# Cosine attention and a gated feed-forward on one core: batch 2's preparation moved into chunk 0's second product, and three evictions moved between ScalarE and VectorE

## The chip, the cores and the metric

The kernel runs on one core of a Trainium2 chip. The metric is device time in microseconds, the median over runs of one program. Each of the core's engines works through its own queue in order: TensorE (PE; its weight loads are PEld), VectorE (DVE), ScalarE (ACT), GpSimd (POOL, which here issues the loads and clears small pieces), and SyncE (SP, which issues the stores and the transposing DMAs).

## The reference

```python
def _attn_ref(q, k, v):                       # 8 batches, 8 heads, 576 positions, 64 wide
    theta = np.pi / 2.0 * pos / S
    q_p = phi(q, cos_w, sin_w)                # relu(q)*cos next to relu(q)*sin: 128 wide
    k_p = phi(k, cos_w, sin_w)
    kv = np.einsum('bhsf,bhsd->bhfd', k_p, v)
    z = np.sum(k_p, axis=2)
    num = np.einsum('bhsf,bhfd->bhsd', q_p, kv)
    den = np.einsum('bhsf,bhf->bhs', q_p, z)[..., None] + 1e-06
    return num / den

def _moe_ref(x, w_in, w_out):                 # x: the 4608 tokens, 512 wide
    h = x @ w_in                              # 512 x 2048
    return (h * np.cos(h)) @ w_out            # 2048 x 512
```

## The kernel before

**Tiling.** The 4608 tokens go through the feed-forward in nine chunks of 512 (`NCHUNK`). A chunk has a first product of 16 groups (`m1_group`: four matmuls into M, then ScalarE's `co` = sin(M + pi/2) and VectorE's `g` = M * co) and a second product of 4 tiles of 128 tokens, each in four parts of four matmuls (`m2_part`; after the last part ScalarE copies the tile to `ost`, and SP stores it). Chunk 0 does its first product in two halves of 256 tokens. A batch has 576 tokens, so chunk 1 needs all of batch 0 and most of batch 1.

**Attention** is done batch by batch, a little ahead of the chunk that needs it:

- `loads(b)`: three DMAs from POOL into q16, k16, v16 (two buffers each)
- `scaled(b, which, i)`: two VectorE instructions per sixth i, relu and times cos or sin, into `kp` or `qp` (one buffer each)
- `spread_v`: four ScalarE copies that lay v out with a column of ones, `vz`, which POOL sets first (batches from 1 on)
- `kv_head`: six matmuls per head into KV; ScalarE copies four heads at a time to `kvz`
- `q_turn`: turns qp into `X`. For batches 0 and 1 by matmuls into `QT` that ScalarE copies out (batch 1: two sixths at a time); for later batches by a transposing DMA on SP
- `num_tile(b, t)`: eight matmuls into `NP` for 128 tokens, then VectorE's dn, rd and x
- `x_turn(b, t)`: turns x into `XT`, the input of the first product; by matmuls into `XP` and a ScalarE copy for batches 0 and 1, by a transposing DMA for later ones

**The order** is written out by hand. `at(c, s, f, ...)` puts a step behind place s of chunk c; places 0 to 15 are the first product and 16 to 31 the second (chunk 0: 0 to 31 and, from z = 32 on, 32 to 47). Every engine's queue holds its instructions in that order. Before the first chunk stands a prologue with the whole of batch 0's preparation; in it, matmuls on zeros (`warm`, tile W) stand between steps.

**Buffers in PSUM.** Pool `psA` has two buffers for KV, QT of batch 1, NP and XP of batch 1 (tag "att"); pool `psM` has two for tag m1 and two for m2, for M, for QT and XP of batch 0 and for the tiles of the second product. Which buffer an allocation gets, and so for whom it waits, is settled when the program is built.

Of the kernel before, what the change touches and what calls it, by code (L numbers as in the profile page):

```python
# [10 lines left out]
AF = mybir.ActivationFunctionType  # L11
ALU = mybir.AluOpType
F32 = mybir.dt.float32
F16 = mybir.dt.float16
# [3 lines left out]
def kernel(  # L18
# [9 lines left out]
    nc = tc.nc  # L28
    B, H, S, D = q.shape
    Dm, Dff = moe_w_in.shape  # L30
    P = 128
    F = 2 * D
    R = 6
    PR = S // R
# [4 lines left out]
    NCHUNK = NTOK // CH  # L39
    NSUB = CH // P  # L40
# [18 lines left out]
    psA = ctx.enter_context(tc.tile_pool(name="psA", bufs=2, space=bass.MemoryType.PSUM))  # L59
    psM = ctx.enter_context(tc.tile_pool(name="psM", bufs=2, space=bass.MemoryType.PSUM))  # L60

    CS = cpool.tile([PR, 2, R], F32, name="CS")
# [37 lines left out]
    def scaled(b, which, i, h0=0, h1=H):  # L100
        s = st[b]
        if which + "p" not in s:
            s[which + "p"] = apool.tile([PR, R, H * F], F16, name=which + "p",
                                        tag=which + "p", bufs=1)
        dst = s[which + "p"][:, i].rearrange("p (h t d) -> p h t d", t=2, d=D)
        src = s[which + "16"][:, 0:H * RUN].rearrange("p (h i d) -> p h i d", i=R, d=D)
        for t in range(2):
            nc.vector.tensor_scalar(  # L108
                out=dst[:, h0:h1, t, :], in0=src[:, h0:h1, i, :],
                scalar1=0.0, scalar2=CS[:, t, i:i + 1],  # L110
                op0=ALU.max, op1=ALU.mult,
            )

    def q_turn(b, i, tag="m1"):
        s = st[b]
        if i == 0:
            s["X"] = apool.tile([P, H, S], F16, name="X", tag="X")
        if b >= 2:
            nc.sync.dma_start_transpose(
                out=s["X"][:, :, i * PR:(i + 1) * PR], in_=s["qp"][:, i],  # L120
            )
            return
        if b == 1:
            if i % 2 == 0:
                s["QT"] = psA.tile([P, 2, H, P], F16, name="QT", tag="att")
            QT = s["QT"][:, i % 2]
        else:
            QT = psM.tile([P, H, P], F16, name="QT", tag=tag)
        for h in range(H):
            nc.tensor.matmul(  # L130
                QT[:, h, 0:PR], lhsT=s["qp"][:, i, h * F:(h + 1) * F], rhs=ID[0:PR, 0:PR],
                is_transpose=True,
            )
        if b == 1 and i % 2 == 0:
            return
        i0 = i - (b == 1)
        dst = s["X"][:, :, i0 * PR:(i + 1) * PR]
        if b == 1:
            nc.scalar.activation(
                out=dst.rearrange("p h (a c) -> p a h c", a=2),  # L140
                in_=s["QT"][:, :, :, 0:PR], func=AF.Copy,
            )
        else:
            nc.scalar.activation(out=dst, in_=QT[:, :, 0:PR], func=AF.Copy)  # L144

# [64 lines left out]
    def x_turn(b, t):  # L210
        x = st[b]["x", t]
        new = min(P, S - t * P)
        n0 = b * S + t * P
        if b >= 2:
            nc.sync.dma_start_transpose(out=XT[:, :, n0:n0 + new], in_=x[P - new:P, :])
            return
        if b == 0:
            XPf = psM.tile([P, 1024], F16, name="XP", tag="m1")
        else:
            XPf = psA.tile([P, 2048], F16, name="XP", tag="att")  # L220
        XP = XPf[:, 0:NCT * P].rearrange("p (i c) -> p i c", c=P)
        for i in range(NCT):
            nc.tensor.matmul(  # L223
                XP[:, i], lhsT=x[:, i * P:(i + 1) * P], rhs=ID,
                is_transpose=True,
            )
        nc.scalar.activation(out=XT[:, :, n0:n0 + new], in_=XP[:, :, P - new:P], func=AF.Copy)  # L227
# [19 lines left out]
    def m2_part(c, m, part):  # L247
        if part == 0:
            tag = "m1" if c == 0 and m >= 2 else "m2"
            st["m2", m] = psM.tile([P, Dm], F32, name="M2", tag=tag)  # L250
        M2 = st["m2", m]
        for j in range(4 * part, 4 * part + 4):
            nc.tensor.matmul(  # L253
                M2, lhsT=st["g", c][:, j, m * P:(m + 1) * P], rhs=w_out_sb[:, j],
                start=(j == 0), stop=(j == NJT - 1),
            )
        if part < 3:
            return
        ost = opool.tile([P, Dm], F32, name="ost", tag="ost")
        nc.scalar.activation(out=ost, in_=M2, func=AF.Copy)  # L260
        n = c * CH + m * P
        r = 0
        while r < P:
            b, rem = divmod(n + r, S)
            i, p = divmod(rem, PR)
            cnt = min(P - r, PR - p)
            rows = out[b * S:(b + 1) * S, :].rearrange("(p i) d -> p i d", i=R)
            nc.sync.dma_start(out=rows[p:p + cnt, i, :], in_=ost[r:r + cnt, :])
            r += cnt
# [3 lines left out]
    def at(c, s, f, *args):  # L273
        plan.setdefault((c, s), []).append((f, args))

    HS = NJT
    M2S = NJT
# [6 lines left out]
    def plan_stage0():  # L284
        at(0, 1, q_turn, 0, 4)
        at(0, 2, x_turn, 0, 2)
        at(0, 3, q_turn, 0, 5)
        at(0, 6, num_tile, 0, 3)
        at(0, 10, num_tile, 0, 4)
        at(0, 12, x_turn, 0, 3)  # L290
        at(0, HS, x_turn, 0, 4)
        z = 2 * HS
        for i in range(R):
            at(0, z + i // 2, scaled, 1, "k", i)
            at(0, z + 4 + i // 2, scaled, 1, "q", i)
        for n in range(4):
            at(0, z + 1 + n, spread_v, 1, 2 * n)
        for h in range(H):
            at(0, z + 4 + h // 4, kv_head, 1, h)
        for i, n in enumerate((6, 6, 7, 7, 8, 8)):  # L300
            at(0, z + n, q_turn, 1, i)
        for n, f, t in ((9, num_tile, 0), (10, num_tile, 1), (11, x_turn, 0),
                        (11, num_tile, 2), (12, x_turn, 1), (13, num_tile, 3),
                        (14, x_turn, 2), (15, x_turn, 3), (16, num_tile, 4)):
            at(n // 16, n % 16 + (0 if n > 15 else z), f, 1, t)
        at(1, 3, x_turn, 1, 4)
        for i in range(R):
            at(i // 3, i % 3 + (0 if i > 2 else z + 13), scaled, 2, "q", i)
            at(i // 3, i % 3 + (0 if i > 2 else z + 13), q_turn, 2, i)

    def plan_ahead(c, b):
        for i in range(R):
            at(c, M2S + 1 + 2 * i, scaled, b, "q", i)
            at(c, M2S + 1 + 2 * i, q_turn, b, i)
        for i in range(R):
            if i < 3:
                at(c, M2S + 10 + 2 * i, scaled, b, "k", i)
            else:
                at(c + 1, 2 * i - 5, scaled, b, "k", i)
        for n in range(4):  # L320
            at(c, M2S + 8 + 2 * n, spread_v, b, 2 * n)
        for h in range(H):
            at(c + 1, 12 + h // 4, kv_head, b, h)

    def plan_tiles(c, b, s0):
        for t in range(NT):
            at(c, s0 + 2 * t, num_tile, b, t)
            at(c, s0 + 2 * t, x_turn, b, t)

    plan_stage0()  # L330
    at(1, 0, loads, 3)
    for i in range(R):
        at(1, 3 + 2 * i, scaled, 2, "k", i)
    for n in range(4):
        at(1, 2 + 3 * n, spread_v, 2, 2 * n)
    for h in range(H):
        at(1, 14 + h // 4, kv_head, 2, h)
    at(1, M2S, loads, 4)
    plan_tiles(1, 2, M2S + 2)
    plan_ahead(1, 3)  # L340
    for c in range(2, NCHUNK):
        if c + 3 < B:
            at(c, 12, loads, c + 3)
        if c + 1 < B:
            plan_tiles(c, c + 1, M2S)
        if c + 2 < B:
            plan_ahead(c, c + 2)
# [5 lines left out]
    with tc.manual_schedule():  # L353
# [24 lines left out]
        def warm(n):  # L378
            for _ in range(n):
                nc.tensor.matmul(W, lhsT=WU[:, 0:P], rhs=WU, start=True, stop=True)  # L380

        warm(29)
        for i in range(R):
            scaled(0, "k", i, 0, 4)
        for i in range(2):
            scaled(0, "q", i)
            q_turn(0, i)
            warm(2)
        for i in range(R):
            scaled(0, "k", i, 4, 8)  # L390
        for h in range(4):
            kv_head(0, h)
        warm(2)
        for h in range(4, 8):
            kv_head(0, h)
        for i in range(2, 4):
            scaled(0, "q", i)
            q_turn(0, i, ("m1", "m2")[i % 2])
        warm(1)
        num_tile(0, 0)  # L400
        warm(2)
        num_tile(0, 1)
        warm(3)
        x_turn(0, 0)
# [6 lines left out]
        for s in range(2 * HS):  # L411
            n = s // HS * (CH // 2)
# [45 lines left out]
```

## Time and profile before

| | |
|---|---|
| median of 3 runs | 307.33 us (307.19 to 307.38) |
| the profiled execution | 307.16 us |
| its span | 305.4 us |
| PE, DVE, ACT busy | 293.5, 192.4, 164.6 us |
| first matmul of chunk 0's first product (L234) | 20.13 us |
| first matmul of chunk 0's second product (L253) | 38.73 us |
| first matmul of chunk 1's first product | 59.54 us |
| end of it in the chain of waits | 78.19 us |
| last eviction (L260) | 300.92 us |

Times are microseconds from the start of the span. A line such as L234 is a line of the kernel before. A group "out<-in" names tiles: `M<-XT,w_in_sb` is the first product, `M<-w_out_sb,g` the second. A wait names what released the instruction last. In the chain of waits each step is what the next one waited for, so only work in the chain sets the end.

### The profile page before, as it was taken

The numbers are of one execution on the slowest core, as the hardware profiler recorded it, in microseconds if no ns is written. First come the engines' busy times: TensorE is split into PE (matmuls) and PEld (weight loads), VectorE is DVE, ScalarE is ACT, GpSimd is POOL, SyncE is SP. The second block draws the span as 40 slices with busy tenths as digits, with TensorE's granted clock in tenths as the row PEclk, the third lists the DMA queues.
The fourth block names the chain that finished last, engine by engine and source line by source line (L and its number), as shares of the span: only waits on it lengthen the run. The fifth ranks groups of instructions, "written<-read, shape, count | busy, mean of one in ns | idle before, by whom it ended". The sixth has DMA issues, their size and how long they took to land.

```text
span 305.4 us, 5574 instructions
## 1 busy us (share of the span) xinstructions
PE 293.5 (96%) x2101; PEld 153.6 (50%) x2101; DVE 192.4 (63%) x486; ACT 164.6 (54%) x261; POOL 29.1 (10%) x47
## 2 busy tenths in 40 slices
PE   8799999898999999999999999999999999999994
PEld 3567856444554554455445544554455444444441
DVE  2868892599459778577757775777576257108600
ACT  1268956587246735673567256725672167227511
POOL 8433103010101201020102000000000000000000
PEclk9999999999999999999999999999999999999999
DMA  7999999997999976996699676228621520121022
GB/s 99 193 205 206 204 205 204 240 205 103 144 167 145 217 130 140 177 173 118 138 155 204 109 121 146 63 43 125 148 57 36 121 63 0 34 69 38 0 69 69
DMA packets 73483, 38.81 MB, mean 127 GB/s; under 512 B 46320, under 2 KB 68848, under 8 KB 73456
## 3 DMA queue, kind: packets, MB, share of 16 engines
q0 software_dynamic: 23856, 18.35, 40.9%
q1 hardware_dynamic: 49600, 20.10, 32.2%
q8 instruction: 16, 0.26, 0.3%
q14 instruction: 11, 0.09, 0.1%
HBM read 36.74 MB, written 9.44 MB: 151 GB/s over the span
## 4 chain that ended last, share of the span: by engine, by line
PE 84%; DVE 9%; DMA 2%; ACT 2%; issue 1%; POOL 0%; ACTq 0%; POOLq 0%
PE M L253 40%; PE M L234 33%; DVE g L243 6%; PE KV L165 4%; PE NP L191 3%; DMA q<-in_q_dram 2%; PE QT L130 1%; ACT co L240 1%; DVE kp L108 1%; PE W L380 1%; DVE x L204 1%; PE KV L175 1%; DVE qp L108 1%; ACT XT L227 1%; PE XP L223 0%
## 5 line engine op out<-in xcount | busy, mean ns | idle before, releaser
L243 DVE TENSOR_TENSOR g<-M,co 128x512 f16<-128x512 f32 (+1 forms) x160 | 99.5, 634 | 64.5 <-ACT co L240 64.3
L253 PE MATMUL M<-w_out_sb,g 128*128 128x512 f16 x576 | 132.4, 379 | 0.1
L234 PE MATMUL M<-XT,w_in_sb 128*128 128x512 f16 (+1 forms) x640 | 130.2, 358 | 2.3 <-ACT XT L227 1.5
L240 ACT ACTIVATE co<-M,PIH 128x512 f32<-128x512 f32 (+1 forms) x160 | 101.9, 644 | 28.0 <-PE M L234 26.7
L234 PEld LDWEIGHTS <-w_in_sb 128*128 128x128 f16 x640 | 61.5, 98 | 62.4 <-issue 4.3
L253 PEld LDWEIGHTS <-g 128*128 128x128 f16 x576 | 53.6, 98 | 58.2 <-issue 0.3
L260 ACT ACTIVATE ost<-M 128x512 f32<-128x512 f32 x36 | 21.5, 597 | 86.3 <-PE M L253 72.8
L108 DVE TENSOR_SCALAR kp<-k,CS 96x512 f16<-96x512 f16 (+1 forms) x108 | 30.4, 348 | 4.9 <-DMA k<-in_k_dram 4.9
L204 DVE TENSOR_TENSOR x<-NP,rd 128x512 f16<-128x512 f32 x40 | 27.6, 691 | 3.8 <-DMA XT<-x 2.0
L108 DVE TENSOR_SCALAR qp<-q,CS 96x512 f16<-96x512 f16 x96 | 28.6, 347 | 1.1 <-DMA q<-in_q_dram 1.1
L152 ACT ACTIVATE vz<-v 96x768 f16<-96x768 f16 x28 | 22.0, 830 | 0.0
L191 PEld LDWEIGHTS <-X 128*128 128x128 f16 x320 | 15.5, 98 | 8.7 <-DVE x L204 0.3
L198 DVE TENSOR_SCALAR dn<-NP 128x8 f32<-128x8 f32 x40 | 6.5, 163 | 19.5 <-PE NP L191 18.8
L191 PE MATMUL NP<-kvz,X 128*128 128x65 f16 x320 | 16.9, 194 | 0.1
L165 PEld LDWEIGHTS <-kp 96*128 96x128 f16 x336 | 12.7, 98 | 5.0 <-DVE kp L108 1.6
L87 POOL DMA_DIRECT2D q<-in_q_dram x9 | 7.9, 880 | 76.5 <-DVE qp L108 74.1
L165 PE MATMUL KV<-vz,kp 96*128 96x65 f16 x336 | 13.3, 193 | 1.5 <-DVE kp L108 1.5
L380 PE MATMUL W<-WU 128*128 128x512 f16 x45 | 12.7, 419 | 1.2 <-DVE PIH L357 1.2
L180 ACT ACTIVATE kvz<-KV 128x260 f16<-128x260 f32 x16 | 6.2, 387 | 8.3 <-PE KV L165 5.1
L87 POOL DMA_DIRECT2D k<-in_k_dram x9 | 6.9, 764 | 37.0 <-DVE kp L108 33.8
L144 ACT ACTIVATE X<-QT 128x768 f16<-128x768 f16 x6 | 4.7, 808 | 9.2 <-PE QT L130 9.1
L202 DVE RECIPROCAL rd<-dn 128x8 f32<-128x8 f32 x40 | 8.1, 203 | 1.4
(22 smaller groups left out, 53.5 us busy)
## 6 DMA issues: line engine op xcount, KB each, us to landing
out_dram<-ost SPq DMA_DIRECT2D x24, 192.0 KB, 2.4
k<-in_k_dram POOLq DMA_DIRECT2D x7, 576.0 KB, 7.9
v<-in_v_dram POOLq DMA_DIRECT2D x7, 576.0 KB, 10.1
q<-in_q_dram POOLq DMA_DIRECT2D x7, 576.0 KB, 8.5
out_dram<-ost SPq DMA_DIRECT2D x24, 128.0 KB, 2.4
w_in_sb<-in_moe_w_in_dram POOLq DMA_DIRECT2D x4, 512.0 KB, 14.7
w_out_sb<-in_moe_w_out_dram POOLq DMA_DIRECT2D x4, 512.0 KB, 19.9
out_dram<-ost SPq DMA_DIRECT2D x24, 64.0 KB, 2.0
```

Of the source, the lines that this page charges most:

```text
L87: nc.gpsimd.dma_start(out=dst[:, h0:h1, i0 * D:i1 * D], in_=src[b].rearrange("h (p i) d -> p h (i d)", i=R)[:, h0:h1, i0 * D:i1 * D],)
L108: nc.vector.tensor_scalar(out=dst[:, h0:h1, t, :], in0=src[:, h0:h1, i, :], scalar1=0.0, scalar2=CS[:, t, i:i + 1], op0=ALU.max, op1=ALU.mult,
L152: nc.scalar.activation(out=s["vz"][:, h:h + 2, :, 0:D], in_=src[:, h:h + 2], func=AF.Copy,)
L165: nc.tensor.matmul(s["KV"][:, h, 0:n], lhsT=s["kp"][:, i, h * F:(h + 1) * F], rhs=s["vz"][:, h, i, 0:n], start=(i == 0), stop=(i == R - 1),)
L191: nc.tensor.matmul(NP[:, h // 4, o:o + D + 1], lhsT=s["X"][:, h, c0:c0 + P], rhs=s["kvz"][:, h], start=True, stop=True,)
L204: nc.vector.tensor_tensor(out=x.rearrange("p (a h e) -> p a h e", a=2, e=D), in0=np4[:, :, :, 0:D], in1=rd.broadcast_to((P, 2, 4, D)), op= ...
L234: nc.tensor.matmul(M1[:, n0:n1], lhsT=w_in_sb[:, i, j * P:(j + 1) * P], rhs=XT[:, i, c * CH + n0:c * CH + n1], start=(i == 0), stop=(i == ...
L240: nc.scalar.activation(out=co[:, n0:n1], in_=M1[:, n0:n1], func=AF.Sin, bias=PIH, scale=1.0,)
L243: nc.vector.tensor_tensor(out=st["g", c][:, j, n0:n1], in0=M1[:, n0:n1], in1=co[:, n0:n1], op=ALU.mult,)
L253: nc.tensor.matmul(M2, lhsT=st["g", c][:, j, m * P:(m + 1) * P], rhs=w_out_sb[:, j], start=(j == 0), stop=(j == NJT - 1),)
L260: nc.scalar.activation(out=ost, in_=M2, func=AF.Copy)
L380: nc.tensor.matmul(W, lhsT=WU[:, 0:P], rhs=WU, start=True, stop=True)
```

## The change

- Prologue: both halves of batch 0's k are scaled ahead of q; of the second half (heads 4 to 7) the sine part is six ScalarE instructions. q_turn 2 stands between the two groups of kv_head, q_turn 3 behind them, and five of the `warm` matmuls are gone.
- q_turn 4 and 5 and x_turn 2 to 4 of batch 0 use psA instead of psM.
- The second of batch 1's three X copies is done by VectorE.
- Batch 1's steps in chunk 0's second product come one place earlier, and batch 2's q, two thirds of its k and its v are prepared there, not in chunk 1's first product; its last two k steps come at places 3 and 6 of chunk 1, its kv_head at 10 and 11 (14 and 15 before).
- From chunk 1 on the steps stand at the places of the general rule; before, chunk 1 had places of its own (its num_tile two places later, its loads at 16 instead of 12).
- The right half of the last tile is copied by VectorE, the left by ScalarE.

```diff
@@ scaled
+            if b == 0 and which == "k" and h0 == 4 and t == 1:
+                nc.scalar.activation(
+                    out=dst[:, h0:h1, t, :], in_=src[:, h0:h1, i, :], func=AF.Relu,
+                    scale=CS[:, t, i:i + 1],
+                )
+                continue
@@ q_turn
+        elif i >= 4:
+            QT = psA.tile([P, 2, H, P], F16, name="QT", tag="att")[:, 0]
...
-        if b == 1:
+        if b == 1 and i == 3:
+            nc.vector.tensor_copy(
+                out=dst.rearrange("p h (a c) -> p a h c", a=2),
+                in_=s["QT"][:, :, :, 0:PR],
+            )
+        elif b == 1:
@@ x_turn
-        if b == 0:
+        if b == 0 and t < 2:
@@ m2_part
-        nc.scalar.activation(out=ost, in_=M2, func=AF.Copy)
+        if c == NCHUNK - 1 and m == NSUB - 1:
+            nc.vector.tensor_copy(out=ost[:, Dm // 2:], in_=M2[:, Dm // 2:])
+            nc.scalar.activation(out=ost[:, 0:Dm // 2], in_=M2[:, 0:Dm // 2], func=AF.Copy)
+        else:
+            nc.scalar.activation(out=ost, in_=M2, func=AF.Copy)
@@ plan_stage0
-            at(0, z + 4 + i // 2, scaled, 1, "q", i)
+            at(0, z + 3 + i // 2, scaled, 1, "q", i)
...
-        for n, f, t in ((9, num_tile, 0), (10, num_tile, 1), (11, x_turn, 0),
-                        (11, num_tile, 2), (12, x_turn, 1), (13, num_tile, 3),
-                        (14, x_turn, 2), (15, x_turn, 3), (16, num_tile, 4)):
-            at(n // 16, n % 16 + (0 if n > 15 else z), f, 1, t)
-        at(1, 3, x_turn, 1, 4)
         for i in range(R):
-            at(i // 3, i % 3 + (0 if i > 2 else z + 13), scaled, 2, "q", i)
-            at(i // 3, i % 3 + (0 if i > 2 else z + 13), q_turn, 2, i)
+            at(0, z + 8 + i // 2, scaled, 2, "q", i)
+            at(0, z + 8 + i // 2, q_turn, 2, i)
+        for n, f, t in ((8, num_tile, 0), (9, num_tile, 1), (10, x_turn, 0),
+                        (10, num_tile, 2), (11, x_turn, 1), (12, num_tile, 3),
+                        (13, x_turn, 2), (14, x_turn, 3), (15, num_tile, 4)):
+            at(0, z + n, f, 1, t)
+        at(1, 2, x_turn, 1, 4)
+        at(0, z + 9, loads, 3)
+        for i in range(4):
+            at(0, z + 13 + i // 2, scaled, 2, "k", i)
+        at(1, 3, scaled, 2, "k", 4)
+        at(1, 6, scaled, 2, "k", 5)
+        for n in range(4):
+            at(0, z + 11 + n, spread_v, 2, 2 * n)
+        for h in range(H):
+            at(1, 10 + h // 4, kv_head, 2, h)
@@ behind plan_stage0()
-    at(1, 0, loads, 3)
-    for i in range(R):
-        at(1, 3 + 2 * i, scaled, 2, "k", i)
-    for n in range(4):
-        at(1, 2 + 3 * n, spread_v, 2, 2 * n)
-    for h in range(H):
-        at(1, 14 + h // 4, kv_head, 2, h)
-    at(1, M2S, loads, 4)
-    plan_tiles(1, 2, M2S + 2)
-    plan_ahead(1, 3)
-    for c in range(2, NCHUNK):
+    for c in range(1, NCHUNK):
@@ the prologue
-        for i in range(R):
-            scaled(0, "k", i, 0, 4)
+        for h0 in (0, 4):
+            for i in range(R):
+                scaled(0, "k", i, h0, h0 + 4)
         for i in range(2):
             scaled(0, "q", i)
             q_turn(0, i)
-            warm(2)
-        for i in range(R):
-            scaled(0, "k", i, 4, 8)
+            warm(1)
         for h in range(4):
             kv_head(0, h)
-        warm(2)
+        scaled(0, "q", 2)
+        q_turn(0, 2)
+        scaled(0, "q", 3)
         for h in range(4, 8):
             kv_head(0, h)
-        for i in range(2, 4):
-            scaled(0, "q", i)
-            q_turn(0, i, ("m1", "m2")[i % 2])
+        q_turn(0, 3, "m2")
         warm(1)
         num_tile(0, 0)
-        warm(2)
+        warm(1)
```

## The prediction

> **What bounds the kernel now.** I read first the engine totals of the page.
>
> ```profile
> PE 293.5 (96%) x2101; PEld 153.6 (50%) x2101; DVE 192.4 (63%) x486; ACT 164.6 (54%) x261; POOL 29.1 (10%) x47
> ```
>
> PE at 96% doesn't say where time can be won, since a matmul's span overlaps the next one's. The chain of waits in order of time does (start, length, what):
>
> ```profile
> 75.20 0.54 DVE kp L108 x2
> 75.79 0.78 PE KV L165 x19
> 76.56 0.87 PE M L234 x4
> 77.43 0.77 PE KV L165 x24
> 78.19 2.59 PE M L253 x12
> ...
> 93.31 11.22 PE M L234 x52
> ...
> 123.76 11.22 PE M L234 x52
> ```
>
> From 78.19 us on the chain is PE alone until 300.92: each chunk takes 123.76 - 93.31 = 30.45 us, and nothing can be won there. What can be won lies before 78.19 and after 300.92. Busy time by stretch (length; then PE, PEld, DVE, ACT, POOL) shows the two that matter most:
>
> ```profile
> 38.70:46.10 7.40, 7.37 (x75) 4.16 (x75) 7.14 (x26) 4.10 (x7) 0.00 (x0) 1.00 1.27 205
> 46.10:51.10 5.00, 5.00 (x67) 3.44 (x66) 0.00 (x0) 3.70 (x3) 2.49 (x4) 1.00 1.31 203
> 51.10:59.50 8.40, 7.30 (x73) 4.18 (x70) 5.80 (x18) 5.10 (x9) 0.00 (x0) 1.00 1.27 230
> 59.50:78.20 18.70, 16.76 (x125) 8.46 (x125) 14.96 (x37) 13.75 (x22) 2.48 (x3) 1.00 0.94 148
> ```
>
> In chunk 1's first product (59.50 to 78.20) VectorE is the bound: between 60.6 and 75.8 the chain runs over g and the scalings of batch 2. In chunk 0's second product VectorE lies idle from 46.10 to 51.10. The timeline shows the idle time and its end (start, us, what, [idle before]), with the last eviction:
>
> ```profile
> 11.35 1.58 ACT L144 ACTIVATE X<-QT 128x768 f16<-128x768 f16 x2 [9.10 <-PE QT L130]
> 11.39 2.50 DVE L108 TENSOR_SCALAR kp<-k,CS 96x256 f16<-96x256 f16 x12
> 47.20 4.54 ACT L139 ACTIVATE X<-QT 128x1536 f16<-128x1536 f16 x3 [1.16 <-PE QT L130]
> 51.42 0.17 DVE L198 TENSOR_SCALAR dn<-NP 128x8 f32<-128x8 f32 x1 [5.57 <-PE NP L191]
> 300.92 0.60 ACT L260 ACTIVATE ost<-M 128x512 f32<-128x512 f32 x1 [2.91 <-PE M L253]
> ```
>
> Below, the waits of the changed kernel are those that stand in its instruction order; the durations are rows of before.
>
> **Part 1, the prologue.** Before, PE's own work sets it from kv_head 0 (12.52 in the chain) to the first num_tile (16.53): twice 1.34 for 24 KV matmuls, 0.43 for two dummies, 0.68 for q_turn 2 and 3, 0.22 for a dummy, and small waits. The change scales both halves of k first. VectorE ends the first half at 6.08 + 2.95 = 9.03, then does 6 scalings at 2.50/12 = 0.21: 10.29, which is 0.17 after q landed (10.12). Its four scalings of q take 1.35 as before, to 11.64; q_turn 1 runs to 12.03, one dummy to 12.25, kv_head 0 to 3 to 13.59, q_turn 2 (0.34) to 13.93, kv_head 4 to 7 to 15.27 (15.63 before), q_turn 3 and a dummy to 15.83. There num_tile 0 starts, 0.70 earlier; its other gate, the copy of the second kvz, ends at 15.27 + 0.15 + 0.39 = 15.81. From there num, dn, rd and x (1.13 from 16.83 to 17.96), the transposes and the copies of XT are the chain of before. **-0.70** (-0.4 to -0.9; v of heads 4 to 7 lands at 4.2 + 9.0 = 13.2, before its use at 13.9).
>
> The six scalings on ScalarE have no row. The nearest are 0.39 (kvz, 128x260) and 0.47 us (co, 128x256): 2.3 to 2.8 us from the landing of that half of k (issue 2.02 + 5.4 = 7.4). At the dearer end they are done at 10.2 and needed at 13.9, hidden in the 9.10 us for which ScalarE idles; without that cover they would cost up to 2.8. The Trainium skill (ScalarE: Activation LUTs, Rules for kernel authors) says to put relu and mul on VectorE, not on ScalarE; were these on the path, the sum would lose 6 x (0.47 - 0.21) = 1.6 us by it, but the idle row says they are not.
>
> **Part 2, chunk 0's first product (20.13 to 38.73).** q_turn 4, 5 and x_turn 2 to 4 take a psA buffer instead of one of the two m1 buffers. ScalarE's work and order stay, and it is near its limit: 32 co at 0.44, two X at 0.75, three XT at 0.6, 0.6 and 0.4 make 17.2 of 18.6 us. It idles 0.22, 0.35, 0.32 and 0.16 before 26.09, 27.79, 30.48 and 32.32. The second is VectorE's (num_tile 3 stands ahead of g) and stays; around the others PE waits for m1 buffers that a turn holds. Of their 0.70 I take **-0.5** (0 to -0.9).
>
> **Part 3, chunk 0's second product and chunk 1's first.** Times are on before's clock: PE ends q_turn 3 of batch 1 at 48.71 and q_turn 5 at 50.26. VectorE's copy of that X pair (no row: 1536 elements out of PSUM; between 6 x 0.27 = 1.6 by the scalings and 3 x 0.69 = 2.1 by x; g's 0.42 for 256 and 0.68 for 512 give 1.0 ns an element, so 1.7) runs from 48.75 to 50.45. Queued behind it are the scalings of batch 2's q, which wait for q_turn 5 anyway. num_tile 0 reuses the copy's buffer: 50.5 (0.26). M2 takes 0.86. num_tile 1 reuses the last X pair's buffer, freed by ScalarE at 51.75 as before: 51.8. M2 to 52.92, x_turn 0 to 53.2; num_tile 2 now reuses x_turn 0's buffer and waits for ScalarE's XT 0 (0.6): 53.87. M2 and x_turn 1 to 55.3. VectorE meanwhile does four scalings (1.1) and one num chain (1.13) per step: x 1 at 54.98, x 2 at 57.23, x 3 at 58.36, each just in time. num_tile 3 waits for XT 1: 56.45. Three M2 and x_turn 2 and 3 to 59.8, num_tile 4 to 60.06. ScalarE has ost, XT, two vz (0.76 each, new here), ost, XT, vz ahead of XT 3, which ends at 60.55. Chunk 1 needs it and starts at 60.6, not 59.54: **+1.06**. Its first product then holds 16 x 0.864 for M, 1.53 for KV, 0.28 for x_turn 4: 15.63 on PE, with 16 x 0.64 + 4 x 0.27 = 11.3 on VectorE and some 12 on ScalarE, so PE sets it. It ends at 76.23 instead of 78.19: **-1.96** for both. A copy of 2.1 would add 0.4; without the wait for XT 0 it is 0.7 better.
>
> The queues: loads of batch 3 are issued at 46.15 in both, since their buffers set that. On POOL the memset of vz for batch 2 now stands behind them, at about 49, with vz needed at 56. Batch 4's loads go out earlier, as q and k are scaled earlier, and are due in chunk 2. Batch 2's own loads land at 25.94 + 21.2 = 47.1 (q), 28.56 + 21.5 = 50.1 (v) and 30.78 + 22.2 = 53.0 (k), ahead of 50.4, 56.4 and 58.4. On SP two of batch 2's six transposes (1.35 each) now stand ahead of the first output, which lands near 60; ScalarE's fourth ost reuses its buffer at 61.3, with co and a buffer of chunk 1 behind it. num_tile of batch 2 comes two steps earlier, in the order of every later chunk. All of this: 0.
>
> **Part 4, the last tile.** ScalarE's half waits for VectorE's, both being in one buffer: 0.40 (g, 256 wide: 0.42) + 0.08 + 0.39 (kvz) = 0.87 against 0.60. **+0.27** (-0.2 if they overlapped).
>
> **Sum**: -0.70 - 0.50 - 1.96 + 0.27 = -2.9 us. The profiled execution took 307.16 us, 305.4 of span and 1.8 around it, 0.17 under the median of 307.33. So 304.3 on its scale and 304.4 on the median's.
>
> **Rivals.** (a) VectorE's bound only moves. In three steps of part 3 VectorE has 2.2 us of work against 1.4 of PE; if each chain slips, PE waits in chunk 0 what chunk 1 saves. For: x 1 has no slack, x 2 0.3. Against: the idle 5.57 us and the M2 steps that PE has in between. Then parts 1, 2 and 4 are left: 306.4.
> (b) PE cools in the prologue. The trace has seven dummies 0.43 apart up to 4.16 and 0.21 after that: half speed, then full. With fewer dummies from 9.1 to 16 PE could fall back for as long as that first stretch, 3 us, and lose half: 306.0. Against: two dummies fewer by 12.3 is 0.43 us of 3. The Trainium skill (TensorE: Matmul & The Clock Gate, Part 1) states that one idle window of about 3.4 us halves the clock; the longest idle stretch here is 1.9 us by part 1.
> (c) Slower: k of batch 2 lands late. VectorE takes eight of its scalings (2.2 us) ahead of x 4 and of every g of chunk 1, so a late k holds up x_turn 4 and PE. On the clock after parts 1 and 2 they start at 57.2 and could start at 58.7 at no cost; each us after that costs one. k lands at 53.0; two transposes and an output ahead of it may add 4. From 61.6 on, 8.6 later than now, it is slower than before; at 62.4 it gives 308.2.
> (d) The edits of part 2 bring nothing: 304.9, inside the range.
>
> **How the numbers follow.** No change can be told from a change within 0.2%, 0.6 us. Forecast with (d) 0.65, (a) 0.17, (b) 0.08, (c) 0.10. The forecast's own costs span 303.3 (each part near its good end) to 305.6; to leave out no more than 2 in 10 the range goes on over (b) and (a): 303.3 to 306.6. Faster, under 306.7: the forecast, (b) and two thirds of (a), 0.84. Same: the rest of (a) and a mild (c), 0.07. Slower: 0.09.
>
> **What would show it.** Right: the first M L234 near 19.4 and M L253 near 37.5 (lines of before); from 59.4 to 75.0 a chain of PE alone, with no kp or g; ScalarE's last ost after one of VectorE. Wrong: dn and x of batch 1 releasing PE again and again between 49 and 59 (a); dummies or KV at twice their time near 12 us (b); kp waiting for a DMA near 57 (c). A first product of chunk 1 longer than 16.5 us would break part 3.

## The result, and the profile after

The changed kernel takes 309.81 us (309.34 to 310.52, four runs), against 307.26 for the kernel before in the same comparison: a ratio of 1.0084, interval 1.0063 to 1.0105. It is slower by 2.5 us where 2.9 us of gain was forecast, and lies outside the range. The profiled execution took 310.02 us, its span 308.2.

In the listing of the changed kernel the first product's M is L247, the second's L266, ost L277 (the halves of the last tile L274 and L275), co L253, XP L236, the store L285, the transposes of qp L125. The engine totals hardly moved:

```profile
PE 294.5 (96%) x2096; PEld 153.8 (50%) x2096; DVE 192.8 (63%) x482; ACT 165.3 (54%) x266; POOL 29.3 (10%) x47
```

The chain of waits (start, length, what) tells where the time is:

```profile
53.50 0.57 SPq L285
...
54.12 10.35 DMA out_dram<-ost
...
64.58 0.61 ACT ost L277
...
65.22 1.86 PE M L247 x4
67.09 0.43 PE XP L236 x4
67.52 7.45 PE M L247 x32
...
80.82 0.86 PE M L266 x4
```

A store stands in it, for 10.35 us. It is the first tile of chunk 0. ScalarE's fourth ost writes over the first one's buffer, so it waits for that store. That ost in turn frees the buffer in which the third group of chunk 1 is to be built, and the co of the first two groups are queued behind it on ScalarE. So TensorE stops after two groups (58.37 to 60.26) and starts again at 65.22. The view of waits between 45 and 82 us (engine, line, released by: us, times, longest) has both links:

```profile
ACT ost L277 <- DMA out_dram<-ost: 5.5, 1, 5.5
PE M L247 <- ACT ost L277: 5.0, 1, 5.0
```

SP's timeline, with what it issued, shows why the store is late:

```profile
49.28 4.17 SPq L125 DMA_TRANSPOSE X<-qp  x2
53.50 1.80 SPq L285 DMA_DIRECT2D out_dram<-ost  x2
55.34 13.78 SPq L125 DMA_TRANSPOSE X<-qp  x4
```

Two transposes are issued ahead of it. Before, the stores of the first three tiles came first, and only the fourth tile's stood behind two transposes:

```profile
52.26 5.29 SPq L268 DMA_DIRECT2D out_dram<-ost  x6
58.13 2.70 SPq L119 DMA_TRANSPOSE X<-qp  x2
60.92 0.99 SPq L268 DMA_DIRECT2D out_dram<-ost  x2
```

The DMA view (issued between 50 and 54 us; KB each, median us from issue to landing), first after, then before:

```profile
out_dram<-ost SPq DMA_DIRECT2D x1, 192.0 KB, 10.7
```

```profile
out_dram<-ost SPq DMA_DIRECT2D x1, 192.0 KB, 5.4
```

The same store takes twice as long to land behind the transposes. They are slow themselves: the second one is issued near 50.7 and lands 12.8 us later, at 63.5; the tile's 192 KB (53.50 + 10.7) land at 64.2, its last 64 KB at 64.5. The two stretches that follow (length; PE, PEld, DVE, ACT, POOL; granted clock, DMA share, GB/s) show the price:

```profile
59.50:65.20 5.70, 0.76 (x4) 0.24 (x3) 0.09 (x1) 0.62 (x2) 0.00 (x0) 0.99 1.26 213
65.20:80.80 15.60, 15.58 (x109) 7.82 (x109) 10.37 (x19) 11.12 (x18) 1.74 (x3) 0.89 1.06 181
```

In the first, every compute engine is nearly idle. In the second TensorE never stops, but at a granted clock of 0.89: four matmuls take 1.86 us at 65.22 and four of XP 0.43, twice the 0.86 and the 0.22 that four matmuls and XP take in the chain of the first experiment below. From 95.93 on a chunk takes 30.45 us again, as before.

### The profile page after: what moved, and what is told of

It reads as the page before. It is cut to its first block, busy times and chain, and to the rows that moved or that the text cites. A ratio compares the mean times of both kernels' runs of the same rounds, so it can differ in the third digit from the quotient of the medians.

```text
span 308.2 us, 5568 instructions
## 1 busy us (share of the span) xinstructions
PE 294.5 (96%) x2096; PEld 153.8 (50%) x2096; DVE 192.8 (63%) x482; ACT 165.3 (54%) x266; POOL 29.3 (10%) x47
## 4 chain that ended last, share of the span: by engine, by line
PE 83%; DVE 7%; DMA 6%; ACT 2%; issue 1%; SPq 0%; ACTq 0%; POOLq 0%
PE M L266 37%; PE M L247 36%; DMA out_dram<-ost 4%; PE KV L178 3%; DVE g L256 3%; PE NP L204 3%; DMA k<-in_k_dram 2%; DVE kp L114 1%; PE QT L138 1%; DVE x L217 1%; DVE qp L114 1%; ACT co L253 1%; PE KV L188 1%; ACT XT L240 0%; ACT ost L277 0%
## 5 line engine op out<-in xcount | busy, mean ns | idle before, releaser
L247 PE MATMUL M<-XT,w_in_sb 128*128 128x512 f16 (+1 forms) x640 | 131.1, 360 | 5.8 <-ACT ost L277 5.0
L266 PE MATMUL M<-w_out_sb,g 128*128 128x512 f16 x576 | 132.4, 379 | 0.1
L253 ACT ACTIVATE co<-M,PIH 128x512 f32<-128x512 f32 (+1 forms) x160 | 102.1, 646 | 29.0 <-PE M L247 28.1
L247 PEld LDWEIGHTS <-w_in_sb 128*128 128x128 f16 x640 | 61.7, 98 | 66.1 <-issue 8.0
L266 PEld LDWEIGHTS <-g 128*128 128x128 f16 x576 | 53.7, 98 | 58.5 <-issue 0.3
L277 ACT ACTIVATE ost<-M 128x512 f32<-128x512 f32 x35 | 20.9, 598 | 88.2 <-PE M L266 69.2
L114 DVE TENSOR_SCALAR kp<-k,CS 96x512 f16<-96x512 f16 (+1 forms) x102 | 28.6, 348 | 4.8 <-DMA k<-in_k_dram 4.8
L396 PE MATMUL W<-WU 128*128 128x512 f16 x40 | 12.8, 465 | 1.2 <-DVE PIH L373 1.2
L274 DVE COPY ost<-M 128x256 f32<-128x256 f32 x1 | 0.4, 424 | 12.5 <-DMA out_dram<-ost 12.5
```

The lines of the kernel that those rows point to most:

```text
L114: nc.vector.tensor_scalar(out=dst[:, h0:h1, t, :], in0=src[:, h0:h1, i, :], scalar1=0.0, scalar2=CS[:, t, i:i + 1], op0=ALU.max, op1=ALU.mult,
L247: nc.tensor.matmul(M1[:, n0:n1], lhsT=w_in_sb[:, i, j * P:(j + 1) * P], rhs=XT[:, i, c * CH + n0:c * CH + n1], start=(i == 0), stop=(i == ...
L253: nc.scalar.activation(out=co[:, n0:n1], in_=M1[:, n0:n1], func=AF.Sin, bias=PIH, scale=1.0,)
L266: nc.tensor.matmul(M2, lhsT=st["g", c][:, j, m * P:(m + 1) * P], rhs=w_out_sb[:, j], start=(j == 0), stop=(j == NJT - 1),)
```

## The experiments

Ratios are to the kernel before, run on the same chip in the same comparison.

**A fourth buffer for ost.** The changed kernel with:

```diff
-        ost = opool.tile([P, Dm], F32, name="ost", tag="ost")
+        ost = opool.tile([P, Dm], F32, name="ost", tag="ost", bufs=4)
```

> The changed kernel with four ost buffers in place of three, so that the fourth ost of chunk 0 reuses nothing. Theory (store): what costs is that this ost waits 5.5 us for the first store, which stands on SP behind two transposes; PE's third group of chunk 1 waits 5.0 us behind it and then runs at half clock, 1.7 us more. Then this kernel has no ACT ost wait on a DMA near 60, chunk 1's first product is PE alone and ends near 75, and the time is 309.8 - 5.0 - 1.7 = 303.1 us. Rival (work): the VectorE and ScalarE work packed into chunk 0's second product is what costs; then the time stays near 309.8, with PE waiting for dn, x or XT in chunk 0. Rival (traffic): the DMA engines are full of batch 3's loads, and the store is late in any order; then this kernel too takes 303.1, but its first store still lands 10 us after its issue.

Measured: 303.48 us (303.27 to 305.2), ratio 0.9883 (0.9853 to 0.9913), span 301.7, clock 1.000. Its chain of waits:

```profile
58.67 2.70 PE M L247 x12
61.38 0.22 PE XP L236 x4
61.60 6.91 PE M L247 x32
...
74.36 0.86 PE M L266 x4
```

TensorE alone, from the start of chunk 1 on; the first product takes 15.69 us instead of 22.45. The store still lands 10.6 us after its issue, and nobody waits for it. One buffer turns the change from 2.5 us slower to 3.7 us faster, so the whole loss hung on that one reuse. VectorE's bound (rival (a)) is ruled out as its cause: nothing else was eased.

**The transposes behind the stores.** The changed kernel, three ost buffers, batch 2's `q_turn` later:

```diff
         for i in range(R):
             at(0, z + 8 + i // 2, scaled, 2, "q", i)
-            at(0, z + 8 + i // 2, q_turn, 2, i)
...
+        for i in range(R):
+            at(0, z + (11 if i < 4 else 13), q_turn, 2, i)
```

> The changed kernel with three ost buffers, and batch 2's transposes issued at places z + 11 and z + 13 instead of z + 8 to z + 10, so that the first store stands ahead of them on SP. Theory (store): the first store goes out at 50.5 and lands within 6 us, as in the kernel before; the fourth ost does not wait; 303.1 us. Rival (traffic): the store lands 10 us after its issue in this order too, near 61, and ost waits some 2 us; 305 us or more. Rival (work): 309.8 us, unchanged.

Measured: 305.19 us (304.37 to 305.85), ratio 0.9925 (0.9898 to 0.9952). That is 2.1 above the 303.1 of the theory and near the 305 of the rival (traffic), but not for that rival's reason: the first store lands 5.7 us after its issue, and TensorE runs through chunk 1's first product. Instead the moved transposes make a wait of their own, which this kernel's chain shows:

```profile
68.97 10.76 DMA X<-qp
...
80.04 0.61 DVE qp L114 x2
...
81.84 0.42 PE NP L204 x8
```

The scaling of batch 3's q writes the only qp buffer and waits for the last of batch 2's transposes to have read it; behind this scaling VectorE's dn, rd and x come late for the next num_tile. In the profiled executions (304.37 and 303.52 us) this is where it falls behind the fourth buffer: it starts chunk 1 0.26 us earlier (58.41 against 58.67), and chunk 2's first product 0.82 later (90.29 against 89.47). The medians lie 1.7 apart; what makes up the rest is open. The early transposes had a use.

**The store from another queue.** The changed kernel, with the first tile's two stores issued by ScalarE instead of SP:

```diff
-            nc.sync.dma_start(out=rows[p:p + cnt, i, :], in_=ost[r:r + cnt, :])
+            eng = nc.scalar if c == 0 and m == 0 else nc.sync
+            eng.dma_start(out=rows[p:p + cnt, i, :], in_=ost[r:r + cnt, :])
```

> The changed kernel, three ost buffers, with the first tile's two stores issued from ScalarE's own DMA queue, so that batch 2's transposes keep their place on SP and the store is not behind them. Theory (order on the queue): the store lands 5 to 6 us after an issue near 50.5, as in e2, and the fourth ost is free when its tile is done; ScalarE's XT 0 comes later by the two issues, so 303.5 to 304.5 us. Rival (sharing): transposes and loads share the DMA engines, so the store takes 10 us on any queue and lands near 61; the fourth ost and PE's third group then wait some 2 us, 305.5 us or more.

Measured: 303.59 us (303.35 to 303.82), ratio 0.9867 (0.9841 to 0.9893). All transposes keep their places on SP, and beside them the store lands thus:

```profile
out_dram<-ost ACTq DMA_DIRECT2D x1, 192.0 KB, 6.5
```

So the traffic that it shares doesn't explain the delay: beside the same transposes and loads it takes 6.5 us, behind two of them 10.7. The Trainium skill (DMA: Bandwidth & Descriptors, Queues, rings and completion order) says that SP and ACT each own a row of rings on the same DMA engines, that a ring is consumed in order, and that an engine takes turns between rows; 6.5 against 10.7 agrees with it.

The place behind two transposes isn't enough either. In the kernel before, the fourth tile's store, issued at 60.92, has that place too. Its DMA view (issued between 58 and 62 us):

```profile
out_dram<-ost SPq DMA_DIRECT2D x1, 192.0 KB, 5.3
X<-qp SPq DMA_TRANSPOSE x2, 6.5
```

There the second transpose lands 6.1 us after its issue near 59.5, and the store at 66.2, 0.6 behind it; in the changed kernel it is 12.8 us and 0.7. So in both the store lands just behind the transposes, and how late that is depends on how long they take. While the two transposes were under way, the packets of GpSimd's loads filled 100% of the DMA engines' time in the changed kernel (49.3 to 63.5) and 47% in the kernel before (58.1 to 65.7). That the loads slow the transposes fits this, but no run varied them alone.

**TensorE kept busy in the wait.** The changed kernel with twenty matmuls on zeros behind chunk 1's second group, in psA buffers:

```diff
+    def hot(n):
+        for _ in range(2):
+            W = psA.tile([P, CH], F32, name="W", tag="att")
+            for _ in range(n // 2):
+                nc.tensor.matmul(W, lhsT=WU[:, 0:P], rhs=WU, start=True, stop=True)
...
+        at(1, 1, hot, 20)
```

> The changed kernel, with twenty matmuls on zeros put into TensorE's queue behind the second group of chunk 1, where it waits 5 us for ScalarE's fourth ost. At full speed they take 20 x 0.216 = 4.3 us, less than the wait. Theory (the wait costs 5.0 us, and another 1.7 because the idle stretch halves the clock for the next 3.4 us): after the wait the matmuls stand 0.22 apart, the rest of the first product takes 13.9 us as without the wait, and the time is 309.8 - 1.7 = 308.1. Rival (the matmuls after the wait are slow because of something else, such as the weights or XT being read beside the transposes): 309.8, with the slow stretch still there. The dummies sit in psA buffers; they could hold up x_turn 4 by no more than their own 4.3 us, which lies inside the wait.

Measured: 308.44 us (307.88 to 308.94), ratio 1.0031 (1.0018 to 1.0045). The wait for the store is there as before, and its chain goes on with:

```profile
64.83 1.02 PE M L247 x4
65.86 0.22 PE XP L236 x4
66.08 6.91 PE M L247 x32
...
78.84 0.86 PE M L266 x4
```

The rest of the first product takes 78.84 - 64.83 = 14.0 us instead of 80.82 - 65.22 = 15.6. In ratios the gain is 0.0053, 1.6 us. So the idle stretch costs twice: 5.0 us of waiting and 1.6 of half speed after it. The Trainium skill (TensorE: Matmul & The Clock Gate, Part 1) says that the clock is halved after at least one idle window of about 3.4 us. The trace agrees: after 5.0 us of idle time the matmuls were at half speed, and with the gap filled they were not.

**The prologue and the psA buffers alone.** The kernel before with the edits of parts 1 and 2:

```diff
+            if b == 0 and which == "k" and h0 == 4 and t == 1:
...
+        elif i >= 4:
+            QT = psA.tile([P, 2, H, P], F16, name="QT", tag="att")[:, 0]
...
-        if b == 0:
+        if b == 0 and t < 2:
...
+        for h0 in (0, 4):
...
```

> The kernel before with the prologue of the change (k first, six scalings on ScalarE, q_turn 2 and 3, five dummies fewer) and the psA buffers of q_turn 4, 5 and x_turn 2 to 4, and nothing else. Forecast of parts 1 and 2: -1.2 us, 306.1 us. From the changed kernel's trace, whose second product of chunk 0 starts at 37.00 instead of 38.73: -1.7 us, 305.5 us, if the rest of the kernel takes the shift over. If chunk 1 is held by loads instead, less.

Measured: 305.53 us (305.19 to 305.92), ratio 0.9938 (0.9918 to 0.9958): 1.7 us faster.

**The psA buffers alone.** Of that diff, only the second and the third piece.

> The kernel before with nothing but psA buffers for q_turn 4, 5 and x_turn 2 to 4 of batch 0. Forecast of part 2: -0.5, 306.7 us. The changed kernel's first product of chunk 0 takes 17.49 us from its first matmul to the second product's, against 18.60 before: -1.1, 306.1 us, if that is these buffers' doing and not the prologue's.

Measured: 306.30 us (306.05 to 306.62), ratio 0.9954 (0.9936 to 0.9972): 1.2 us by the medians. The first product goes from 20.17 to 37.65, 17.48 us, against 18.60 before.

**The moved preparation alone.** The kernel before with VectorE's X copy and the new order of `plan_stage0` and of chunk 1, without parts 1, 2 and 4.

> The kernel before with batch 2's preparation moved and VectorE's copy of the second X pair, and neither the prologue, the psA buffers nor the split last tile. Theory (store): the first store again stands behind two transposes and lands when batch 3's loads end, near 64, whatever the prologue; so chunk 1 ends as late as in the changed kernel, near 80.8, and the time is 309.8 less the 0.27 of the last tile: 309.5 us. Rival (work): the moved work costs what it costs from a later start: 309.8 + 1.7 - 0.3 = 311.2 us. If the forecast's part 3 held: 305.3 us.

Measured: 311.36 us (310.51 to 312.27), ratio 1.0131 (1.0097 to 1.0164): 4.1 us slower. Its waits:

```profile
ACT ost L265 <- DMA out_dram<-ost: 5.0, 1, 5.0
PE M L239 <- ACT ost L265: 4.4, 1, 4.4
```

I had expected the landing to stay fixed near 64 us, and so a shorter wait. It moved along: issued at 55.04, landed at 65.7. What the store waits for is the transposes, and they start when the q that they turn is ready: at 51.04 here, at 49.28 in the changed kernel. The time is the 311.2 of the rival (work), but the waits are those of the store, and the fourth buffer above took the loss away with all the work in place. The 4.4 us for which TensorE idles were enough to slow it down too: from the end of the wait (66.41) to the second product (82.10) it takes 15.7 us, where it takes 14.0 with the wait filled. The loss is all in this part.

**The fourth buffer without the change.** The kernel before with `bufs=4` for ost.

> The kernel before, with four buffers for ost instead of three and nothing else. It tells whether the fourth buffer is worth anything without the change. Theory (the store is only late behind the two transposes that the change puts ahead of it): no stretch of before waits for a store, so 307.3 and no difference that can be measured. Rival (stores hold up ScalarE in other chunks too, and the fourth buffer gives a gain of its own that was counted to the change): 1 us or more faster, 306 or less.

Measured: 307.32 us (306.92 to 309.2), ratio 1.0002 (0.9986 to 1.0019). The buffer has no gain of its own; what it brings above is the cure of this wait.

**The two copies that changed engines.** The fourth buffer, and the last tile by ScalarE alone:

```diff
-        if c == NCHUNK - 1 and m == NSUB - 1:
-            nc.vector.tensor_copy(out=ost[:, Dm // 2:], in_=M2[:, Dm // 2:])
-            nc.scalar.activation(out=ost[:, 0:Dm // 2], in_=M2[:, 0:Dm // 2], func=AF.Copy)
-        else:
-            nc.scalar.activation(out=ost, in_=M2, func=AF.Copy)
+        nc.scalar.activation(out=ost, in_=M2, func=AF.Copy)
```

> e1 with the last tile copied by ScalarE alone, as in the kernel before. Forecast of part 4, 0.27 us for the split: 303.2 us against 303.5. In the trace of the changed kernel the split takes 0.89 us from 303.55 to 304.39, against 0.60 before. If the two halves had helped: 303.7.

Measured: 303.31 us (303.07 to 304.85), ratio 0.9868 (0.9839 to 0.9896). Then also the second X pair of batch 1 by ScalarE again:

```diff
-        if b == 1 and i == 3:
-            nc.vector.tensor_copy(
...
-        elif b == 1:
+        if b == 1:
```

> e6 with the second X pair of batch 1 copied by ScalarE, as in the kernel before. ScalarE is free from 46.92 and the pair is ready at 46.98, so it ends near 48.45, 0.1 us after num_tile 0 could start, and the third pair starts as it did: within 0.2 us of e6. If ScalarE is the limit there: up to 1.45 us more, the length of the copy.

Measured: 303.10 us (303.07 to 303.44), ratio 0.9855 (0.9824 to 0.9885). The intervals of these two and of the fourth buffer alone overlap, and the fourth buffer alone ran in another comparison (the kernel before took 307.23 us there, 307.48 here), so the 0.17 and the 0.21 us between the medians settle nothing; the traces show the tail 0.24 shorter, and no wait that VectorE's copy of X removes: num_tile 1 waits for ScalarE's last X copy with either. This last version has the lowest median of all that ran, 4.4 us below the kernel before, and leaves out two of the changed kernel's edits.

## Why the prediction was wrong

The step that failed is in part 3, under the queues. It named the two transposes (1.35 us each) ahead of the first output, said that this output "lands near 60", that ScalarE's fourth ost reuses its buffer at 61.3 "with co and a buffer of chunk 1 behind it", and priced all of it at 0. Every link of the loss is in that sentence but the landing. Those times are on the clock of before; the second product starts 1.73 us earlier now, so they stand for 58.3 and 59.6. The ost was ready at 59.1, and the store landed at 64.5, 6.2 late. In effect the prediction took the store to cost what it costs alone and the transposes to cost SP their issue time: 52.26 for the first store of before, 2.70 for two transposes and 5.4 to land give 60.4. In the trace the two take 4.17 us to issue, and the store behind them, which lands only behind them, takes 10.7 from its issue. The margin was 1.3 us, the error was not covered, and it was given no rival. Rival (c) did put 4 us on "two transposes and an output ahead", but for the k of batch 2, which comes on POOL's queue and was not late; the victim was the output itself.

The second price had no term either: rival (b) looked for a cooling of TensorE in the prologue, where nothing happened (a dummy takes 0.22 us there, 24 KV matmuls 1.34 as before). It came behind the new wait, and the forecast had none.

The other steps, by the chain of waits of the changed kernel:

- **Part 1:** chunk 0's first matmul at 19.51 instead of 20.13, -0.62 (forecast -0.70). ScalarE's six scalings take 2.50 us, 7.45 to 9.95, hidden as forecast. The gain depends on when q lands, for which the forecast had a margin of 0.17 us: in five of the eight profiled executions with this prologue VectorE waits for q (its scalings start at 10.27 to 10.72, against 10.21 here), and in all eight the first matmul lies between 19.36 and 20.03.
- **Part 2:** the first product takes 17.49 instead of 18.60, -1.11 (forecast -0.5, at most -0.9). This term was mis-sized: the estimate took 0.5 of the 0.70 us for which ScalarE idles in three gaps. It is VectorE's g that ends this product, in a run without a gap: from 33.45 on before (TensorE still stands in the chain at 31.84 and 32.31), from 31.93 on with the buffers alone. The run starts 1.5 us earlier and is one g (0.44) longer, which leaves 1.1. Counting ScalarE's idle rows missed how much earlier VectorE would get to that run.
- **Part 3 without the wait** (fourth buffer): chunk 1 starts 21.42 us after the second product instead of 20.81, +0.61 (forecast +1.06); its first product takes 15.69 (forecast 15.63) instead of 18.65. Together -2.35 (forecast -1.96). The 0.45 is ScalarE's: the prediction put its instructions end to end by their durations, but where there is no wait the next one starts earlier (XT at 56.78, vz at 57.25, though XT lasts 0.59). So ScalarE's XT 3 ends at 58.58, and TensorE's own work, up to 58.67, sets the start. VectorE's X copy took 0.96 us instead of 1.7, and that moved nothing. num_tile 1 to 3 waited for ScalarE's X, XT 0 and XT 1, as forecast.
- **Part 3 as it ran:** the first product took 80.82 - 58.37 = 22.45, of which 6.8 are the wait and the half speed; over the 16.5 us that the prediction gave as the sign that this part is broken.
- **Part 4:** the last tile takes 303.55 to 304.39, 0.84 instead of 0.60: +0.24 (forecast +0.27; the 0.89 in the expectation of the run with the last tile by ScalarE alone should read 0.84). ScalarE's half waits for VectorE's:

```profile
303.55 0.44 DVE ost L274
...
304.01 0.38 ACT ost L275
```

The sum closes: -0.62 - 1.11 on the way to the second product, +0.56 to the start of chunk 1 (58.37 - 37.00 against 20.81), +3.80 in its first product, +0.24 at the end give 2.87 us, and the two profiled executions differ by 310.02 - 307.16 = 2.86. Without the store's wait the forecast of 304.4 would have been 0.9 too high.

## What to carry to other kernels

When a step is moved, its DMAs move with it: list what stands behind them in the same queue, take the landing of those transfers behind the moved ones and not alone, and compare it with the moment when their buffer is written again. A wait of this kind on TensorE's path can have a second price, the slow matmuls after it; here it came after 5.0 and after 4.4 us. A spare buffer, or the other queue, cured this wait at no measured cost; try that before giving up a reordering that is right otherwise.

## What the hardware showed

- The first tile's 192 KB store lands 5.4 to 5.7 us after its issue when it is ahead of the transposes, 6.5 on ScalarE's queue, and 10.2 to 10.7 behind two transposes on SP that take up to 12.8 us themselves. Behind two transposes that take 6.5, the fourth tile's store lands in 5.3.
- SP needed 2.70 us to issue two transposes at 58.13 in the kernel before, 4.17 at 49.28 and 13.78 for the next four in the changed one: their issue has no fixed price.
- After 5.0 us of idle time TensorE's matmuls stood 0.43 us apart, which cost 1.6 to 1.75 us (1.00 in the four of M, 0.21 in XP, 0.54 in the next 32). After 4.4 us it cost 1.7.
- VectorE copied 1536 16-bit elements a partition out of PSUM in 0.96 us, 0.6 ns each, against 0.42 us for g's 256 in 32 bits.
